# Reordering the first loads of a gated mixer kernel: first wk piece at the head of the ACT queue, gate vector second, and one transposed load in two parts

## The chip, the cores and the metric

The kernel runs on one NeuronCore of one Trainium2 chip. The metric is device time in microseconds (us) of a whole execution, as the median of several runs. Before the change it is 262.96 us (three runs, 262.92 to 263.25).

## What is computed

For x of 2048 rows and 640 columns in bfloat16 two blocks are computed and mixed row by row. Block A is a linear attention with 32 heads of 20 columns; block B is a layer norm, a product, a shift of four column groups along the rows, a second product and a two-layer MLP. Cut to what matters:

```python
g = sigmoid((x * gate_w).sum(-1, keepdims=True))
# A: linear attention, phi(t) = where(t > 0, t + 1, exp(t)) + 1e-6
q, k, v = heads(x @ wqkv)
kv = einsum("bhsd,bhse->bhde", phi(k), v);  z = phi(k).sum(rows)
a = (einsum("bhqd,bhde->bhqe", phi(q), kv) / (phi(q) . z + 1e-6)) @ wo
# B: mixer and MLP
h  = gelu(layernorm(x) @ w1)
x1 = x + shifted(h) @ w2
b  = x1 + gelu(layernorm(x1) @ w3) @ w4
out = g * a + (1 - g) * b
```

## The kernel before

The 2048 rows are 16 chunks of 128 rows (NCH), or 4 tiles of 512 (NT). The 640 columns are 5 pieces of 128 (DC). The whole program is one unrolled list with a schedule written out by hand: each engine does its instructions in the order in which the code names them, and semaphores between engines are put in by the framework.

The first stage, up to about 27 us, is the K product with phi. For it TensorE (PE) needs x transposed (xT, the stationary operand) and the five wk pieces (wk_sb, the moving operand). The chunks of xT come in two ways. Chunks 0 and 1 are loaded plainly (load_x, line 120) and transposed on PE by turn (lines 207 to 221): products with the identity for chunk 0, transposes for chunk 1, and a copy out of PSUM by VectorE (DVE), line 218. Chunks 2 to 15 are loaded by transposing DMAs (load_xT, line 123), six of them: chunks 2, 3, 4 to 5, 6 to 7, 8 to 11 and 12 to 15, all on the SP queue.

The gate needs the product of x with gate_w. It is had as one more column of the K product: gate_w is loaded as 5 rows of 128 (g5, line 129), copied by DVE into a zeroed tile (line 201), turned by one small product (line 217, inside turn(0)), and written into column 640 of wk_sb by DVE (line 221). The second half of each K product (hf = 1 in k_mm, line 185, 321 columns) reads that column; the first half (320 columns) does not.

The start is ordered by hand. Two queues issue loads: SP (nc.sync) and ACT (nc.scalar). SP has x chunk 0, wk pieces 1, 3 and 4, then the transposing loads, then wq, the rest of x, wv, w1, six pieces of wo, eight of w2, and w3 (lines 138 to 147). ACT has the gate vector, wk piece 0, x chunk 1 and wk piece 2. Meanwhile PE runs filler products on constants (warmup, line 198): six before turn(0), one after it, and one of 256 columns before the second and before the third wk piece of chunk 0. The wk pieces of chunk 0 are used in the order k0_order (line 192), that is 1, 0, 3, 4, 2, with turn(1) ahead of the fourth. Then the chunks 1 to 15 follow with the pieces in order (lines 232 to 235). Each chunk is evacuated by k_evac: ScalarE (ACT) copies the gate column (line 189) and takes exp (line 177), DVE finishes phi (lines 178 and 179).

The landings of the loads are told by eight semaphores that all DMAs take in turn; a DMA that takes one again waits first until the earlier one with it has landed. The trace shows the eight in this order at the start: gate vector, x chunk 0, wk 0, wk 1, x chunk 1, wk 3, wk 2, wk 4. The first six transposing loads take the first six of them again.

After the K product come the Q product (line 242, needs wq), K transposed times x (line 319), and the mixer and MLP stages (lines 353, 436, 467, 483, 518). w2_sb is first used at line 436.

Of the kernel before, what the change touches and what calls it, by code (L numbers as in the profile page):

```python
# [16 lines left out]
def kernel(  # L17
# [14 lines left out]
    P = 128  # L32
# [12 lines left out]
    CG = D // 4  # L45
# [25 lines left out]
    def pair():  # L71
        return ps.tile([P, 2, 512], F32, name="pp")
# [7 lines left out]
    w2_sb = const.tile([P, DC, D], BF16)  # L80
# [36 lines left out]
    sp, aq, gq = nc.sync, nc.scalar, nc.gpsimd  # L117

    def load_x(c0, c1, q=sp):
        q.dma_start(x_sb[:, c0:c1, 0:D], x2[c0 * P:c1 * P, :].rearrange("(c p) d -> p c d", p=P))  # L120

    def load_xT(c0, c1):
        sp.dma_start_transpose(xT[:, :, c0 * P:c1 * P], x2[c0 * P:c1 * P, :])

    def load_wk(q, dc):
        q.dma_start(wk_sb[:, dc, 0:D], A_wqkv[dc * P:(dc + 1) * P, D:2 * D])

    load_x(0, 1)
    aq.dma_start(g5[:], gate_w.rearrange("(c p) -> c p", p=P))
    load_wk(sp, 1)  # L130
    load_wk(aq, 0)
    load_x(1, 2, aq)
    load_wk(sp, 3)
    load_wk(aq, 2)
    load_wk(sp, 4)
    for c0, c1 in ((2, 3), (3, 4), (4, 6), (6, 8), (8, 12), (12, 16)):
        load_xT(c0, c1)
    sp.dma_start(wq_sb, wqkv_v[:, :, 0:D])
    load_x(2, 16)
# [1 line left out]
    sp.dma_start(w1_sb[:], B_w1.rearrange("(c p) f -> p c f", p=P))  # L141
    for g in range(NG):
        sp.dma_start(wo_sb[:, g, :], A_wo[row0[g]:row0[g] + P, :])
    for g in range(4):
        sp.dma_start(w2_sb[:, g, :], B_w2[CG * g:CG * g + P, :])
        sp.dma_start(w2_sb[32 * g:32 * (g + 1), 4, :], B_w2[CG * g + P:CG * (g + 1), :])
    sp.dma_start(w3_sb[:], B_w3.rearrange("(c p) f -> p c f", p=P))

# [40 lines left out]
        nc.scalar.copy(ylog[:, c:c + 1], pt[:, 1, HD:HD + 1])  # L189
        phi(pk[:, c, :].rearrange("p (h e) -> p h e", h=2), pt[:, :, 0:HD], D)  # L190

    k0_order = (1, 0, 3, 4, 2)
    warm = pair()
    one = nc.const_aps.tensor(1.0, (P, TS), BF16)

# [451 lines left out]
```

## Time and profile before

| what | us |
|---|---|
| median of three runs | 262.96 |
| the runs | 263.25, 262.96, 262.92 |
| profiled execution, whole time | 262.89 |
| its span, first to last instruction | 261.1 |
| PE busy in the span | 257.6 (99%) |
| DVE busy | 141.9 (54%) |
| ACT busy | 82.9 (32%) |
| POOL busy | 27.1 (10%) |

The span stands 1.8 us below the whole time of the same execution. The clock granted to PE is shown as full in every slice, and DMA engines are busy seven to nine tenths in the first four slices of 6.5 us. A line of the timeline has the start and the duration in us, the engine (PEld is PE's weight load, a q behind the name marks the issuing queue), the line of the code, the tiles written and read, and in brackets how long the engine stood idle before it and what ended that. "x6" means that six such instructions are drawn together.

### The profile page before, as it was taken

How to read it: one execution, taken by the hardware profiler on the slowest of the kernel's cores; microseconds unless marked ns; L12 is line 12 of the kernel's file. 1: busy time of each engine (PE TensorE's matmuls, PEld its weight loads, DVE VectorE, ACT ScalarE, POOL GpSimd, SP SyncE). 2: the span in 40 equal slices, each digit the busy share in tenths (PEclk: the TensorE clock that was granted, in tenths of full speed). 3: DMA queues.
4: the chain of work that ended last, by engine and by line, in shares of the span. 5: the costliest groups of instructions: out<-in, count | busy, mean ns of one | idle time of the engine just before them, and what ended most of it. 6: DMA issues, size and time to landing. Idle time of an engine off the chain costs nothing.

```text
span 261.1 us, 4172 instructions
## 1 busy us (share of the span) xinstructions
PE 257.6 (99%) x1670; PEld 159.1 (61%) x1670; DVE 141.9 (54%) x277; ACT 82.9 (32%) x124; POOL 27.1 (10%) x82
## 2 busy tenths in 40 slices
PE   8999999999999999999999999999999999999995
PEld 4777555788754644565676566567745567555543
DVE  2788778899947884967312378970312223112132
ACT  1555554321165346431520311140233350142100
POOL 3000050012220140131000123310000000000000
PEclk9999999999999999999999999999999999999999
DMA  7999987016684826996002011331200001100011
GB/s 205 179 204 377 365 241 306 0 28 126 125 99 88 220 54 145 207 298 60 0 3 75 25 28 25 75 54 25 78 25 0 0 3 50 53 0 0 0 53 50
DMA packets 47265, 25.78 MB, mean 99 GB/s; under 512 B 35214, under 2 KB 46478, under 8 KB 47246
## 3 DMA queue, kind: packets, MB, share of 16 engines
q1 hardware_dynamic: 46804, 25.03, 39.5%
q10 hardware_dynamic: 442, 0.49, 0.5%
q8 instruction: 13, 0.21, 0.4%
q14 instruction: 6, 0.05, 0.1%
HBM read 13.03 MB, written 3.60 MB: 64 GB/s over the span
## 4 chain that ended last, share of the span: by engine, by line
PE 99%; DVE 0%; issue 0%
PE pp L518 22%; PE pp L483 21%; PE pp L185 9%; PE pp L319 8%; PE pp L436 8%; PE pp L467 8%; PE pp L353 8%; PE pp L242 8%; PE pp L198 1%; PE pp L527 1%; PE pp L492 1%; PE pp L386 1%; PE pp L372 1%; PE pp L257 0%; PE pp L215 0%; DVE oc L532 0%
## 5 line engine op out<-in xcount | busy, mean ns | idle before, releaser
L483 PE MATMUL pp<-lnxT,w_sb 128*128 128x512 bf16 x260 | 60.0, 379 | 0.0
L518 PE MATMUL pp<-w_sb,h 128*128 128x384 bf16 (+3 forms) x416 | 57.9, 299 | 0.0
L485 ACT ACTIVATE h<-pp 128x1024 bf16<-128x1024 f32 (+1 forms) x28 | 27.0, 963 | 94.3 <-PE pp L483 94.3
L518 PEld LDWEIGHTS <-h 128*128 128x128 bf16 x416 | 38.3, 98 | 19.4 <-issue 1.2
L483 PEld LDWEIGHTS <-w_sb 128*128 128x128 bf16 x260 | 25.4, 98 | 27.2
L532 DVE SCALAR_TENSOR_TENSOR oc<-pp,omg,x 128x640 bf16<-128x640 f32 (+2 forms) x20 | 14.4, 748 | 45.4 <-PE pp L527 21.2
L470 DVE SCALAR_TENSOR_TENSOR x<-pp,gate,x 128x640 f32<-128x640 f32 x16 | 14.1, 879 | 33.6 <-PE pp L467 33.6
L177 ACT ACTIVATE e<-pp 128x640 bf16<-128x640 f32 (+1 forms) x26 | 21.5, 827 | 9.6 <-PE pp L242 9.6
L467 PE MATMUL pp<-m_sb,pqT 128*128 128x320 bf16 x160 | 24.3, 299 | 0.0
L436 PE MATMUL pp<-w_sb,hsT 128*128 128x320 bf16 x160 | 23.5, 299 | 0.0
L185 PE MATMUL pp<-wk_sb,xT 128*128 128x320 bf16 (+1 forms) x160 | 23.0, 302 | 0.0
L319 PE MATMUL pp<-x_sb,pk 128*128 128x320 bf16 (+1 forms) x160 | 22.0, 300 | 0.0
L242 PE MATMUL pp<-xT,hsT 128*128 128x512 bf16 x100 | 21.7, 379 | 0.0
L319 PEld LDWEIGHTS <-pk 128*128 128x128 bf16 x160 | 18.8, 117 | 3.2
L436 PEld LDWEIGHTS <-hsT 128*128 128x128 bf16 x160 | 15.6, 98 | 7.7
L467 PEld LDWEIGHTS <-pqT 128*128 128x128 bf16 x160 | 15.7, 98 | 7.7
L289 POOL TENSOR_SCALAR rstd<-mv 128x1 f32<-128x1 f32 (+1 forms) x20 | 7.7, 386 | 115.4 <-DVE mv L295 115.4
L185 PEld LDWEIGHTS <-xT 128*128 128x128 bf16 x160 | 15.6, 99 | 6.5 <-DVE xT L218 0.2
L439 DVE TENSOR_TENSOR x<-pp,x_sb 128x640 f32<-128x640 f32 x16 | 13.1, 816 | 10.6 <-PE pp L436 10.4
L353 PE MATMUL pp<-lnxT,w_sb 128*128 128x512 bf16 x80 | 18.1, 379 | 0.0
L242 PEld LDWEIGHTS <-hsT 128*128 128x128 bf16 x100 | 11.8, 118 | 9.7
L179 DVE SCALAR_TENSOR_TENSOR pk<-pp,e 128x640 bf16<-128x640 f32 x16 | 13.2, 825 | 1.7
(75 smaller groups left out, 191.1 us busy)
## 6 DMA issues: line engine op xcount, KB each, us to landing
x_sb<-in_A_x_dram SPq DMA_DIRECT2D x1, 2240.0 KB, 11.2
out_dram<-oc SPq DMA_DIRECT2D x14, 160.0 KB, 1.8
w_sb<-in_B_w_dram SPq DMA_DIRECT2D x1, 2160.0 KB
w_sb<-in_B_w_dram SPq DMA_DIRECT2D x1, 2080.0 KB, 11.7
wo_sb<-in_A_wo_dram SPq DMA_DIRECT2D x6, 160.0 KB, 7.3
m_dram<-x SPq DMA_DIRECT2D x3, 320.0 KB, 2.9
hsT<-in_A_wqkv_dram SPq DMA_DIRECT2D x1, 800.0 KB
m_sb<-in_A_wqkv_dram SPq DMA_DIRECT2D x1, 800.0 KB
```

The lines of the kernel that those rows point to most:

```text
L177: nc.scalar.activation(ev, src, ACT.Exp)
L185: nc.tensor.matmul(pt[:, hf, 0:n], lhsT=xT[:, dc, c * P:(c + 1) * P], rhs=wk_sb[:, dc, hf * HD:hf * HD + n], start=(dc == first), stop=(dc ...
L242: nc.tensor.matmul(pt[:, t % 2, :], lhsT=wq_sb[:, dc, :].rearrange("p (m j) -> p j m", j=DC)[:, j], rhs=xT[:, dc, t * TS:(t + 1) * TS], st ...
L319: nc.tensor.matmul(pt[:, hf, 0:HD + hf], lhsT=w, rhs=x_sb[:, c, hf * HD:(hf + 1) * HD + hf], start=(c == 0), stop=(c == NCH - 1))
L353: nc.tensor.matmul(pt[:, i, :], lhsT=w, rhs=lnxT[t][:, dc, :], start=(dc == 0), stop=(dc == DC - 1))
L436: nc.tensor.matmul(pt[:, hf, 0:HD], lhsT=hsT[:, fc, 2 + c * P:2 + (c + 1) * P], rhs=w2_sb[:, fc, hf * HD:(hf + 1) * HD], start=(fc == 0), ...
L467: nc.tensor.matmul(pt[:, hf, 0:HD], lhsT=pqT[:, j, c * P:(c + 1) * P], rhs=m_sb[:, j, hf * HD:(hf + 1) * HD], start=(j == 0), stop=(j == D ...
L470: nc.vector.scalar_tensor_tensor(x1, pt[:, :, 0:HD], gate[:, c:c + 1], x1, op0=ALU.mult, op1=ALU.add)
L483: nc.tensor.matmul(pt[:, k, :], lhsT=w3_sb[:, dc, fc * P:(fc + 1) * P], rhs=lnT[:, dc, :], start=(dc == 0), stop=(dc == DC - 1))
L485: nc.scalar.activation(h2[:, 2 * i * TS:(2 * i + n) * TS], pt[:].rearrange("p h e -> p (h e)")[:, 0:n * TS], ACT.Gelu_apprx_tanh)
L518: nc.tensor.matmul(dst, lhsT=st[t]["h2"][:, fc * TS + cc * P:fc * TS + (cc + 1) * P], rhs=w4_sb[:, fc, a:b], start=start and fc == 0, stop ...
L532: nc.vector.scalar_tensor_tensor(oc[:, a:b], src, omg[:, c:c + 1], st[t]["x1"][cc][:, a:b], op0=ALU.mult, op1=ALU.add)
```

## The change

The ACT queue begins with wk piece 0 instead of the gate vector, which becomes its second load. The order of the loads within SP's queue is the same as before, though their place in the program's text moves. The transposing load of chunks 8 to 11 becomes two, 8 to 9 and 10 to 11. The first two of the eight w2 loads that fill column groups 0 and 1 become one load with the same bytes. Chunk 0 uses wk piece 0 first and wk piece 1 second.

```diff
     load_x(0, 1)
+    load_wk(aq, 0)
+    load_wk(sp, 1)
     aq.dma_start(g5[:], gate_w.rearrange("(c p) -> c p", p=P))
-    load_wk(sp, 1)
-    load_wk(aq, 0)
+    load_wk(sp, 3)
     load_x(1, 2, aq)
-    load_wk(sp, 3)
+    load_wk(sp, 4)
     load_wk(aq, 2)
-    load_wk(sp, 4)
-    for c0, c1 in ((2, 3), (3, 4), (4, 6), (6, 8), (8, 12), (12, 16)):
+    for c0, c1 in ((2, 3), (3, 4), (4, 6), (6, 8), (8, 10), (10, 12), (12, 16)):
         load_xT(c0, c1)
...
+    sp.dma_start(w2_sb[:, 0:2, :], B_w2[0:2 * CG, :].rearrange("(g p) f -> p g f", g=2)[0:P])
     for g in range(4):
-        sp.dma_start(w2_sb[:, g, :], B_w2[CG * g:CG * g + P, :])
+        if g >= 2:
+            sp.dma_start(w2_sb[:, g, :], B_w2[CG * g:CG * g + P, :])
         sp.dma_start(w2_sb[32 * g:32 * (g + 1), 4, :], B_w2[CG * g + P:CG * (g + 1), :])
...
-    k0_order = (1, 0, 3, 4, 2)
+    k0_order = (0, 1, 3, 4, 2)
```

## The prediction, made before the result was known

> **What bounds the kernel now.** I read the busy shares first: PE is busy 257.6 of the 261.1 us span (99%). Then the chain of work that ended last, in order of time, because on such a kernel only a hole in PE's row, or a stretch at the lower clock, can be won or lost. Its start:
>
> ```profile
> 0.83 2.61 PE pp L198 x6
> 3.44 0.53 PE pp L215 x5
> 3.98 0.01 PE pp L217
> 3.98 0.45 PE pp L198
> 4.43 0.27 PE pp L185
> 4.70 0.03 issue
> 4.72 0.43 PE pp L185
> ...
> 6.01 0.28 PE pp L213 x5
> 6.29 21.09 PE pp L185 x154
> 27.38 21.58 PE pp L242 x100
> ```
>
> From 0.83 us to the end PE runs piece after piece. L198 is filler on constants, put where data is awaited. The change leaves each filler in place, so it removes no PE work: it can only close or open waits. Where they are is in the timeline of the first 26 us (start, duration, engine, line; in brackets the idle time before and its releaser):
>
> ```profile
> 0.79 0.57 ACTq L129 DMA_DIRECT2D g<-in_gate_w_dram  x1
> ...
> 2.65 13.64 SPq L123 DMA_TRANSPOSE xT<-in_A_x_dram  x6
> 2.72 0.18 DVE L201 COPY g5z<-g 5x128 bf16<-5x128 bf16 x1 [1.73 <-DMA g<-in_gate_w_dram]
> ...
> 3.06 0.65 PEld L215 LDWEIGHTS <-x_sb 128*128 128x128 bf16 x5 [0.42 <-DMA x_sb<-in_A_x_dram]
> ...
> 3.69 0.89 DVE L218 CAST xT<-pp 128x256 bf16<-128x256 f32 x2 [0.79 <-PE pp L215]
> ...
> 4.50 0.17 DVE L221 CAST wk_sb<-pp 128x5 bf16<-128x5 f32 x1
> ...
> 16.30 9.79 PEld L185 LDWEIGHTS <-xT 128*128 128x128 bf16 x73 [0.16 <-DMA xT<-in_A_x_dram]
> ```
>
> The reader is to see a chain of three arrivals: the gate vector g lets DVE copy it at 2.72; x chunk 0 lets PE load at 3.06; then casts, then L221, which writes the gate column. The second half of the first K product reads that column, and starts at 4.72, right after L221 ends at 4.67. The first half began at 4.22 and takes 0.27, so PE waits some 0.2 us there: the one hole of the start. At 16.30 chunk 8's weights come as its transfer lands, yet the single matmul records around it stay 0.135 us apart (16.05, 16.18, 16.32, 16.46): no hole, but no slack either.
>
> **What the Trainium skill says.** "TensorE: Matmul & The Clock Gate", Part 1, has the array at half rate until about 3.4 us of sustained work have passed. The trace agrees on the rates: 512-column fillers start 0.43 us apart (1.64, 2.06, 2.49), warm 320-column products 0.135. From the gaps between 5.15 and 5.33 the rate doubles near 5.29 us. "DMA: Bandwidth & Descriptors", section on queues, rings and completion order: SP and ACT have a ring each on the same 16 engines, and an engine drains a packet of one ring before it turns to the other. The packet records agree: after the first 160 KB piece, the pieces of both queues pass one after the other, alternating: wk1 (SP), wk0 (ACT, first row 3.19), wk3, x chunk 1, and so on. Two of g's five rows ran at 2.27, when x chunk 0's eight rows on those engines were through. The same page, on issuing engines, says a second queue saves only issue time; so wk0 beside x chunk 0 brings no bandwidth, it takes part of it.
>
> **The change, part by part.**
>
> *wk0 to the head of ACT.* It is issued at 0.79 with x chunk 0, where g was. A 160 KB piece is eight 1280-byte rows on each engine at 0.055 us, 0.44 us. The first touch of the weight tensor costs more: between 2.33 and 2.93 the records hold one slow row for most engines, 0.19 to 0.74 us, as wk1 starts; wk0 will pay that now. Two orders are possible, since the first rows of the two queues stood 0.07 us apart before (1.74 for g, 1.81 for x):
> (a) wk0's rows go ahead of x's on some engine. Then x lands at 3.02 (last landing record) + 0.44 + 0.2 to 0.7, or 3.7 to 4.2. Load and matmul follow within 0.1, and the filler ended near 3.28: PE and the casts are 0.5 to 1.0 us late.
> (b) x goes first. Then x is on time, but see g.
>
> *g second on ACT.* In (b) it stands behind wk0, perhaps wk1 too. The second ACT transfer had its first row at 3.19 before; one more piece makes 3.7. A landing came 0.31 us after its row (g: 1.74 and 2.05), so g lands at 3.5 to 4.0, not 2.62. The wait is L201's on DVE, with the L218 casts and L221 queued behind; L217 on PE waits for its copy, with the filler and every K product behind it. Copy start comes 0.1 after landing, its end 0.18 later: casts can start at 3.8 to 4.3 instead of 3.69, 0.1 to 0.6 late. Before, this wait was hidden under the arrival of x (2.90 against 3.06); that cover is what the move spends.
>
> I take 0.5 us late for either order; the ends are 0.1 and 1.0. Below zero isn't to be had here: x isn't issued earlier, and the hole before 4.72 ends with L221, behind the same casts.
>
> *What 0.5 us late costs.* The second half of the first product starts at 5.22 instead of 4.72. After 5.29 everything runs at the double rate. Until chunk 1's transposes are through, PE has: this half (0.17, part of it cold), filler 0.11, two products 0.27, filler 0.11, two products 0.27, five transposes 0.28. 5.22 + 1.21 = 6.43, against 6.29 before: **+0.14 us**. The idle half microsecond replaces cold work that is then done warm. With 0.1 late it is about +0.05 (half); with 1.0 late all of it is warm: 5.72 + 1.18 = 6.90, +0.6.
>
> *k0 order (0, 1, ...).* Same ten products. wk1 landed at 4.06, 0.16 ahead of its use at 4.22; wk0 takes that place, issued 0.45 us earlier. Without that margin a landing 0.3 late would cost 0.15 at the cold rate. In the trace it is covered: nothing.
>
> *Lanes on SP.* Eight landing semaphores serve all transfers in turn, and a transfer waits for the earlier one of its lane: the first transpose (chunk 2) shares g's, landed at 2.62, issued at 2.65. With wk0 at ACT's head I expect it to wait for wk0 instead, to 3.5 to 4.1. The other transposes, wq and x's bulk are queued behind. The last landings of the transposes were 7.10, 7.95, 9.81, 12.32, 16.26 and 18.34. With chunk 1 starting at 6.29 + 4 x 0.136 = 6.83 and 1.36 us per chunk, chunks 2, 3, 4, 6, 8 and 12 are wanted at 8.19, 9.55, 10.91, 13.62, 16.34 and 21.77: slack 1.1, 1.6, 1.1, 1.3, 0.1, 3.4. Transpose packets started only at 5.4, behind wk4, so most of the 0.9 to 1.5 us of later issue vanishes in that backlog. Nothing for all but chunk 8.
>
> *Split of chunks 8 to 11.* One more transpose issue, about 2 us for two chunks instead of 4.08 for four; SP has time (wq landed at 21.40, wanted at 27.38). Chunks 8 and 9 land near 14.3 instead of 16.26: it gives chunk 8 the slack that the later issue takes. In the profiled execution the gain is 0; uncovered, the late issue would cost up to 1 us there.
>
> *w2 in one transfer less.* One SP issue of 0.33 us less near 30 us, used from 85.97: nothing. With the split it keeps the number of transfers, so later lanes stay.
>
> Sum: +0.14. The profiled execution took 262.89 (261.1 span, 1.8 around it), which gives 263.03; it stands 0.07 below the median 262.96, so against the median it is **263.1**. A measurement of this kernel can tell about 0.2% from no change, 0.53 us: 262.43 to 263.49.
>
> **The rivals.**
> 1. *The moves change nothing on the path* (chance 0.20). x goes first and g goes ahead of wk1, landing by 3.4. For it: the casts need g only by about 3.4. Against: the second ACT transfer never started before 3.19. Time 262.9, or 262.8 if the hole before 4.72 shrinks.
> 2. *The clock comes a window later: slower* (0.14). Up to 5.29 PE idles about 0.2 us; with the change 0.6 to 0.7. If the monitor asks for more work than that leaves, the rate doubles 3.4 us later, by the clock page's window: 3.4 us at half rate lose 1.7 us. It decides at a threshold that no view shows. Against: the fillers still cover four fifths. Time 264.7.
> 3. *The transposes lose their backlog* (0.10). If SP's wait of up to 1.5 us passes through whole, chunk 2 or 4 lands 0.4 late on top of a start that is 1.0 late: 263.0 + 0.6 + 0.3, so 263.5 to 263.9. Against: packets before 5.4 were queued, not starved.
> 4. *Faster by more than can be told* (0.06). The three runs span 0.33 us; if that is chunk 8 or wk1 coming late without the profiler, the split and the order save it, and with the hole closed the time is 262.4. Against: the profiled execution, without such a wait, is already the fastest.
>
> **Numbers.** Forecast 0.50, of which 0.04 beyond 263.49 (1.0 late). Faster 0.06; same 0.46 + 0.20 = 0.66; slower 0.04 + 0.14 + 0.10 = 0.28. The range takes in the forecast with both ends, rivals 1 and 3: 262.5 to 263.9; left out are the clock and the gain, 0.20.
>
> **What would show it.** After the change the idle time before L215's load should grow from 0.42 to nearly 1 us, or L201's start should move from 2.72 past 3.6; L221 should end near 5.2; the first transpose issue should start after 3.3; no idle time before chunk 8's loads; chunk 1 should start near 7.0. L221 ending at 4.7 makes rival 1 right. A run of L185 products 0.27 apart after 5.5 makes rival 2 right. Idle time at chunks 2 to 7 is rival 3. I am wrong altogether if PE's fillers or products end earlier than now.

## The result, and the profile after

The changed kernel takes 263.84 us (median of five runs, 263.67 to 264.21) against 262.93 of the kernel before on the same chip (five runs, 262.70 to 263.25): ratio 1.0033, 95% interval 1.002 to 1.0047. Measured twice more (c1 and e1 below), each time beside the kernel before, it gave 1.0014 (1.0001 to 1.0027) and 1.0033 (1.0016 to 1.0051). The time lies in the stated range, but the forecast was +0.14 us and no measurable change; it is +0.9 us here and +0.5 and +0.6 in the repeats, slower. The runs of one kernel scatter over about 1 us, with a few beyond.

The profiled execution took 264.21 us, its span 262.5. The profile before, of 262.89 us, is of a quick execution: of 145 later runs of that kernel 10 were as quick, and their median was 263.24. So the two profiles differ by more than the two kernels do in the median. In the changed code the gate load is line 131 instead of 129, and the lines of the computing part stand two later (L185 is L187, L215 is L217, L218 is L220, L221 is L223). The timeline of its first 26 us:

```profile
0.79 0.40 ACTq L126 DMA_DIRECT2D wk_sb<-in_A_wqkv_dram  x1
...
0.79 0.40 SPq L120 DMA_DIRECT2D x_sb<-in_A_x_dram  x1
...
1.21 0.58 ACTq L131 DMA_DIRECT2D g<-in_gate_w_dram  x1
...
3.83 14.43 SPq L123 DMA_TRANSPOSE xT<-in_A_x_dram  x7
3.92 0.18 DVE L203 COPY g5z<-g 5x128 bf16<-5x128 bf16 x1 [2.94 <-DMA g<-in_gate_w_dram]
4.05 0.45 PEld L217 LDWEIGHTS <-x_sb 128*128 128x128 bf16 x5 [1.41 <-DMA x_sb<-in_A_x_dram]
...
4.49 0.89 DVE L220 CAST xT<-pp 128x256 bf16<-128x256 f32 x2 [0.38 <-PE pp L217]
...
5.29 0.17 DVE L223 CAST wk_sb<-pp 128x5 bf16<-128x5 f32 x1
```

Each arrival is later: g's copy 2.72 to 3.92, x's load 3.06 to 4.05, the casts 3.69 to 4.49, the gate column 4.50 to 5.29. The landing records say the same: wk 0 at 3.82, g at 3.82, x chunk 0 at 4.00 (3.02 before). Here wk 0's rows went ahead: ACT's ring had its first row at 1.82 and 14 rows started before SP's first at 2.04. The first transposing load was issued at 3.83, right after wk 0 landed.

The chain of waits for the first 20 us:

```profile
0.79 3.21 DMA x_sb<-in_A_x_dram
4.00 0.05 issue
4.05 0.72 PE pp L217 x5
...
5.51 0.43 PE pp L187
5.94 0.21 PE pp L200
6.15 0.53 PE pp L187 x2
6.69 0.21 PE pp L200
6.90 0.53 PE pp L187 x2
7.43 0.30 PE pp L215 x5
7.74 12.26 PE pp L187 x90
```

Before, the chain ran over PE's fillers from 0.83; now its first 4 us are the load of x. And the pieces after it are slow: two products take 0.53 as late as 6.90. Before, two took 0.27 already here:

```profile
5.36 0.27 PE pp L185 x2
```

The rate doubled near 7.3, not near 5.3. Of the +1.34 us at the start of chunk 1 (6.78 before, 8.12 now, by single records) 0.79 came with the data: the first product started at 5.01 instead of 4.22. The other 0.55 came with the clock. Nothing is given back later: the whole time less the start of chunk 1 is 256.11 us before and 256.09 after. In all profiles below that reach full rate by then, but one (a6), it is 256.06 to 256.11, so the start of chunk 1 is the quantity to explain.

### The profile page after: what moved, and what is told of

Its sections match the earlier page's. It is cut to its first block, busy times and chain, and to the rows that moved or that the text cites. A ratio compares the mean times of both kernels' runs of the same rounds, so it can differ in the third digit from the quotient of the medians.

```text
span 262.5 us, 4153 instructions
## 1 busy us (share of the span) xinstructions
PE 257.3 (98%) x1652; PEld 159.4 (61%) x1670; DVE 141.9 (54%) x277; ACT 82.8 (32%) x124; POOL 26.7 (10%) x82
## 4 chain that ended last, share of the span: by engine, by line
PE 97%; DMA 1%; issue 0%; DVE 0%
PE pp L520 22%; PE pp L485 21%; PE pp L187 9%; PE pp L321 8%; PE pp L438 8%; PE pp L469 8%; PE pp L244 8%; PE pp L355 8%; DMA x_sb<-in_A_x_dram 1%; PE pp L529 1%; PE pp L494 1%; PE pp L388 1%; PE pp L374 1%; PE pp L259 0%; PE pp L200 0%
## 5 line engine op out<-in xcount | busy, mean ns | idle before, releaser
L187 PE MATMUL pp<-wk_sb,xT 128*128 128x320 bf16 (+1 forms) x160 | 23.5, 306 | 0.0
L187 PEld LDWEIGHTS <-xT 128*128 128x128 bf16 x160 | 15.8, 100 | 6.4 <-DVE xT L220 0.2
```

The lines of the kernel that those rows point to most:

```text
L187: nc.tensor.matmul(pt[:, hf, 0:n], lhsT=xT[:, dc, c * P:(c + 1) * P], rhs=wk_sb[:, dc, hf * HD:hf * HD + n], start=(dc == first), stop=(dc ...
```

## The experiments

In the diffs below, lines are those of the kernel named first. "Full rate" is read from the gaps between single matmul records.

**a1_gate_first: the changed kernel with the ACT order of before.**

```diff
+    aq.dma_start(g5[:], gate_w.rearrange("(c p) -> c p", p=P))
+    load_wk(sp, 1)
     load_wk(aq, 0)
-    load_wk(sp, 1)
-    aq.dma_start(g5[:], gate_w.rearrange("(c p) -> c p", p=P))
```

> The changed kernel with the gate vector back at the head of the ACT queue and wk piece 0 second; the split, the w2 merge and the piece order (0, 1, ...) stay. Theory A (wk piece 0 ahead of x chunk 0 on the DMA engines makes x late, and the idle PE also gets its full clock later): x lands near 3.0 us again, no idle time before the first transposes, full rate near 5.3; 262.9 to 263.1 us, at most 0.1 to 0.2 over the kernel before, because the first product now waits for wk piece 0, which landed at 4.37 before and is used at 4.22. Theory B (the loss comes from the other edits: the split, the later transposes, the piece order): stays near 263.8.

Measured: 263.26 us, ratio 0.9997 (0.9982 to 1.0013). x landed at 2.96. The loss is gone when the two loads on ACT are swapped back; split, w2 merge and piece order don't cost it. Its profile also shows what the new piece order risks, on PE's timeline:

```profile
3.84 0.59 PE L200 MATMUL pp<-const-bfloat16-1.0 128*128 128x512 bf16 x1
5.13 0.43 PE L187 MATMUL pp<-wk_sb,xT 128*128 128x320 bf16 x2 [0.70 <-DMA wk_sb<-in_A_wqkv_dram]
```

wk 0, wanted first and issued second on ACT, landed at 5.09. Here the rate had doubled by 5.13 already (two products in 0.43), so the moment at which the clock changes differs between executions.

**a2_swap_only: the kernel before with the ACT order changed, nothing else.**

```diff
+    load_wk(aq, 0)
+    load_wk(sp, 1)
     aq.dma_start(g5[:], gate_w.rearrange("(c p) -> c p", p=P))
-    load_wk(sp, 1)
-    load_wk(aq, 0)
```

> The kernel before with only the ACT order changed: wk piece 0 first, gate vector second. Theory A: x chunk 0 lands near 4.0, full rate near 7.3, the whole loss of the change: 263.7 to 264.0. On top of it chunk 8 may wait, since the four-chunk transpose is issued about 1 us later and PE is only 0.8 to 1.4 late itself: 0 to 0.3 more. Theory B: 262.9 to 263.1.

Measured: 263.99, ratio 1.003 (1.0015 to 1.0044): the change's own loss. x landed at 4.11. Six of 22 runs are beyond 264.2, and the profiled one, 265.26, is one of them:

```profile
4.15 0.71 PE L215 MATMUL pp<-ident,x_sb 128*128 128x128 bf16 x5 [0.71 <-DMA x_sb<-in_A_x_dram]
...
6.79 0.74 PE L185 MATMUL pp<-wk_sb,xT 128*128 128x320 bf16 x2
7.33 0.74 PE L213 MATMUL pp<-ident,x_sb 128*128 128x128 bf16 x5
```

Two products in one group show 0.74 at half rate and 0.43 to 0.44 at full rate. Here they are slow past 7, and full rate came near 9.4. Chunk 8 did not wait: its single transposing load landed at 17.02, before PE came to it.

**c1_after_again and e1_after_beside: the changed kernel, unedited, measured again twice.**

> The changed kernel once more, to be compared with the kernels of this call and to see a second profile. Theory A: x chunk 0 lands 0.9 to 1.1 later than in the kernel before, PE idle 0.6 to 0.7 us ahead of the transposes, the full rate anywhere from 6 to 9.5 us; ratio to before 1.002 to 1.004, 0.5 to 1.1 us. Should the full rate come as early as in the kernel before (near 5.3) and the loss be the same, the clock has no part in it.

> The changed kernel beside its variant with more filler, on one chip. So far its median stood 0.49 to 0.91 us over the kernel before, and its two profiles differ: in one the full rate came at 7.3 and PE's own work at half rate set the start of chunk 1 (8.1); in the other it came near 5.2 and the landing of the last wk pieces set it (7.6). I expect 0.5 to 0.9 over before again.

Measured: 263.73, ratio 1.0014 (1.0001 to 1.0027), and 263.76, ratio 1.0033 (1.0016 to 1.0051). Their profiled executions took 263.69 and 263.44, and full rate came near 5.2 and 4.3, as early as in the kernel before or earlier. They are still slower than it. The chain of waits of c1 tells why:

```profile
2.18 4.87 DMA wk_sb<-in_A_wqkv_dram
7.05 0.04 issue
7.09 12.97 PE pp L187 x94
```

The chain no longer goes through x: it is wk 4, landing at 7.05. PE had waited for wk 3 before (landed 6.22) and then stood until 7.09. In e1 wk 4 landed at 6.77. In the kernel before it landed at 6.01 and wk 2, the last piece, at 6.47. So there is a second way to the same loss: with the swap the last first-stage pieces are late too. In seven profiles, with and without the swap (before, a1, b1, c1, d1, e1, e2), chunk 1 starts 0.31 to 0.37 us after the last piece has landed.

**a3_more_filler and e2_filler_beside: the changed kernel with filler up to the landing of x.** Both are the same kernel.

```diff
-    warmup(5)
-    warmup(1, 3 * P)
+    warmup(7)
+    warmup(1, 2 * P)
```

> The changed kernel with more filler ahead of x chunk 0: seven products of 512 columns and one of 256 instead of five and one of 384, so that PE works until 4.03 us, where x lands. It does more PE work than the changed kernel. Theory A, clock part: PE is no longer idle, the full rate comes near 5.3 as before, what follows x runs warm: chunk 1 starts 0.4 later than in the kernel before, not 0.8 to 1.4: 263.2 to 263.4, that is 0.4 to 0.6 less than the change. Rival (the clock comes at a time of its own, whatever PE did): the same time as the changed kernel, 263.7 to 264.0.

> The variant with more filler again (0.34 us over before the first time), now in the same call as the changed kernel. If PE's gap ahead of x takes part in the loss through the clock, it is 0.2 to 0.5 under the changed kernel, with fewer runs beyond 264.2. If the landing of the last wk pieces alone sets the typical run, the two medians agree within 0.1.

Measured: 263.62, ratio 1.0011 (0.9996 to 1.0026), then 263.70 beside 263.76 of the changed kernel, ratios 1.0022 (1.0014 to 1.003) and 1.0033. The medians agree within 0.1; over all measurements none of 27 runs with filler lies beyond 264.2 (highest 264.11), and five of 37 of the changed kernel do (highest 265.51). So no part of PE's gap ahead of x shows in the typical loss. It may make the long runs, but the counts are small, and the kernel before, which in its profile has no such gap, has nine beyond 264.2 in 145. PE stays busy up to the landing of x in the profile of e2, and then waits for its last pieces (wk 4 at 6.89):

```profile
4.05 0.63 PE L217 MATMUL pp<-ident,x_sb 128*128 128x128 bf16 x5
...
6.41 0.44 PE L215 MATMUL pp<-ident,x_sb 128*128 128x128 bf16 x5
6.93 3.16 PE L187 MATMUL pp<-wk_sb,xT 128*128 128x320 bf16 x22
```

Five transposes that start at 6.41 are through within 0.3 of it at this rate (0.28 in the chain of before), and the next product starts at 6.93.

**a4_less_filler and a6_small_gap: the kernel before with less filler, the loads untouched.**

```diff
-    warmup(5)
-    warmup(1, 3 * P)
+    warmup(4)        # a4
+    warmup(5)        # a6
```

> The kernel before with less filler: four products of 512 columns ahead of the transposes and not the one of 384 and the fifth, so that PE is idle from 2.54 us to the landing of x near 3.05. All loads as before, less PE work, and the transposes can start 0.2 earlier than before. Theory A, clock part: the idle half microsecond moves the full rate 1 to 2 us later, which costs 0.3 to 0.9: 263.2 to 263.8. Rival (the clock doesn't follow such a gap): 262.8, 0.1 less than before.

> The kernel before without the filler of 384 columns, so that PE idles only from 2.96 to about 3.1 us. With the run of four fillers only (0.67 idle) the full rate came at 8.3 and the median ratio was 1.002. Theory (a clock window with up to some tenth of idle time still counts as busy): no loss, 0.9995 to 1.0005, full rate at 4 to 7. Rival (any gap ahead of x starts the count again): [...]a ratio of 1.001 to 1.002.

Measured: a4 263.63, ratio 1.0021 (1.0004 to 1.0037), eight of 22 runs beyond 264.2; a6 263.35, ratio 1.0007 (0.9991 to 1.0023). Less work made a4 slower though x landed at 3.17 and the last pieces at 6.24 and 6.42. Its PE timeline in the profiled run (264.2):

```profile
3.21 0.72 PE L214 MATMUL pp<-ident,x_sb 128*128 128x128 bf16 x5 [0.52 <-POOL bmask L163]
...
5.85 0.74 PE L185 MATMUL pp<-wk_sb,xT 128*128 128x320 bf16 x2
6.39 0.74 PE L212 MATMUL pp<-ident,x_sb 128*128 128x128 bf16 x5
6.92 3.14 PE L185 MATMUL pp<-wk_sb,xT 128*128 128x320 bf16 x17
```

There is no wait for data between 4.9 and 8, only half rate, until 8.3. That is the share of the clock by itself. (The releaser named in the bracket is only the last event the profile saw; the weight load beside it waits for x.) For a6 full rate came near 5.7; its interval tells it apart neither from the kernel before nor from a loss of 0.2%. It is the one profile that lost time after the start of chunk 1 (256.53): 0.1 at chunk 8 and 0.36 near 76 us, in a later stage.

**d2_x_second: the kernel before with x chunk 0 behind wk piece 1 on SP.**

```diff
-    load_x(0, 1)
+    load_wk(sp, 1)
     aq.dma_start(g5[:], gate_w.rearrange("(c p) -> c p", p=P))
-    load_wk(sp, 1)
+    load_x(0, 1)
```

> The kernel before with x chunk 0 issued second on SP, behind wk piece 1; the gate vector stays first on ACT, the transposes stay as they were, and no two full pieces start together. x should land at 3.5 to 4.0, as in the changed kernel, but the last wk pieces should land as in the kernel before (6.3 to 6.9). Theory X (what costs is that x is late and PE idle): the loss of the change, ratio 1.002 to 1.0035. Theory L (what costs is that the last wk pieces land later when two pieces start together, and the late x mostly hides behind that): less than half of it, 1.0003 to 1.0012.

Measured: 265.59 (six runs, 263.26 to 266.92), ratio 1.0082 (1.005 to 1.0115). Both theories missed. x landed at 4.52, later than I meant, g in time, the last pieces at 6.17 and 6.60.

```profile
4.57 0.71 PE L215 MATMUL pp<-ident,x_sb 128*128 128x128 bf16 x5 [1.12 <-DMA x_sb<-in_A_x_dram]
...
7.74 0.74 PE L213 MATMUL pp<-ident,x_sb 128*128 128x128 bf16 x5
8.27 2.02 PE L185 MATMUL pp<-wk_sb,xT 128*128 128x320 bf16 x7
```

With PE idle for some 1.3 us and nothing else late, full rate came at 10.1. The profiled execution took 265.82, 2.9 us more than the profile before: 1.30 came with the data (first product at 5.52 instead of 4.22), the rest with the clock. A late x alone thus cost 2.3 us in the median, the larger part through the clock by this split; five of the six runs are 264.96 or longer.

**a5_x1_first: x chunk 1 in wk 0's place at the head of ACT.**

```diff
-    load_wk(aq, 0)
+    load_x(1, 2, aq)
     load_wk(sp, 1)
     aq.dma_start(g5[:], gate_w.rearrange("(c p) -> c p", p=P))
     load_wk(sp, 3)
-    load_x(1, 2, aq)
+    load_wk(aq, 0)
...
-    k0_order = (0, 1, 3, 4, 2)
+    k0_order = (1, 0, 3, 4, 2)
```

> The changed kernel with x chunk 1 at the head of the ACT queue, gate vector second, wk piece 0 third; piece order (1, 0, ...) as before. The same 160 KB stand beside x chunk 0, but from tensor x. Theory A1 (bytes and the slow first touch of the weights both delay x chunk 0): x lands near 3.4 to 3.5, by the bytes alone (0.44), not 4.0; 263.2 to 263.5. Theory A2 (two full pieces that start together are slow, whatever they read): x lands near 4.0, 263.7 to 264.0. In both the gate vector lands past 3.3.

Measured: 265.67 (six runs), ratio 1.0082 (1.0057 to 1.0108). x landed at 3.59 and g at 3.70. The time itself says nothing on the question: wk 0, now third on ACT, landed at 6.50, PE waited 1.0 us for it, and full rate came at 9.4. The landing lies between A1 and A2. With wk 0 beside it x landed at 3.68 to 4.11 (six profiles). Against 3.02 before that is 0.66 to 1.09 later; 0.57 came, in this one profile, with a full piece of x in its place. What the slow first rows add stays open, and they aren't the weights' own: in a3's profile the slow rows at 1.8 to 2.1 (0.35 to 0.77) were x's.

**b1_wk2_on_sp and d1_split_only: two tries for a better version.**

```diff
# b1, from the kernel before
     load_wk(sp, 3)
-    load_wk(aq, 2)
     load_wk(sp, 4)
+    load_wk(sp, 2)
# d1, from the changed kernel
+    aq.dma_start(g5[:], gate_w.rearrange("(c p) -> c p", p=P))
+    load_wk(sp, 1)
     load_wk(aq, 0)
-    load_wk(sp, 1)
-    aq.dma_start(g5[:], gate_w.rearrange("(c p) -> c p", p=P))
...
-    k0_order = (0, 1, 3, 4, 2)
+    k0_order = (1, 0, 3, 4, 2)
```

> A try for a better version: the kernel before with wk piece 2 moved from the end of the ACT queue to SP, behind wk piece 4 and ahead of the transposing loads. In the profile of before PE waits 0.11 us at 6.4 for this piece, which landed at 6.47 while the first transposes ran beside it from 5.4. If the transposes hold it up, it lands 0.1 to 0.3 earlier and the kernel gains 0.1 (ratio 0.9996); if the bytes of all pieces set it, it lands at the same time, and the transposes, issued 0.45 later, may leave chunk 8 waiting up to 0.4: 263.0 to 263.6.

> The kernel before with only the split of the transposing load of chunks 8 to 11 and the merged w2 load; ACT order and piece order as before. In one profile of a kernel with the old single transfer (small gap) the start was quick, chunk 1 began at 6.55, and chunk 8 then waited some 0.4 us for its transfer, which landed at 16.40. Theory: the split pays whenever the start is quick and costs nothing else: chunks 8 and 9 land near 13 to 14.5, no wait; ratio to before 0.9985 to 0.9997, 0.1 to 0.4 us faster. Rival: chunk 8 seldom waits, or the seventh transpose pushes something else: 0.9998 to 1.0003.

Measured: b1 263.23, ratio 1.0005 (0.9997 to 1.0013); d1 263.17, ratio 0.9994 (0.9983 to 1.0005). Neither is told apart from the kernel before. In b1 wk 2 landed at 6.83, not earlier. The ground given for d1 was misread: in a6's profile chunk 1 began at 6.82, not 6.55, and chunk 8 waited about 0.1:

```profile
16.44 1.61 PEld L185 LDWEIGHTS <-xT 128*128 128x128 bf16 x13 [0.26 <-DMA xT<-in_A_x_dram]
```

In d1 chunks 8 and 9 landed at 13.21 instead of 16.26, so the split does give slack; before, that slack was seldom wanted.

## Why the prediction was wrong in its sum, though the time lies in its range

*That the time lies in the range is luck.* The sum reached at most 263.6, with its end of 1.0 us late. Up to 263.9 the range was drawn for rival 3, the transposes, which did not occur.

*x beside wk 0: later, as said.* In the first profile x was the later arrival, in c1 it was g (3.87 against 3.68, copy at 3.97, casts at 4.16). I took 0.5 late; the casts were 0.80 late in the first profile and 0.47 in c1, within the bounds 0.1 to 1.0. But order (b), x first and then on time, never occurred: in c1 and e1 x's ring had its first row first (1.82 against 2.01, 1.83 against 1.95), and x still landed at 3.68 and 3.92. No run delays g alone, so its share in the later casts is read from these profiles only.

*"After 5.29 everything runs at the double rate": this step failed in the first profile.* The sum refunded the idle time with a clock moment copied from one execution. The moment isn't fixed. With x and g ahead and the filler of before, full rate came at 5.3 (before), 5.8 (d1), 6.1 (b1) and by 5.13 (a1); in the unedited changed kernel at 7.3, 5.2 and 4.3. In the first profile the sign named for rival 2, products 0.27 apart after 5.5, is there; it cost 0.55 us, not 1.7. That spread fits "TensorE: Matmul & The Clock Gate", Part 1, of the Trainium skill, which has a free-running window of about 3.4 us. With PE's idle time taken from the starts of its single records, e1's last window would be 0.9 to 4.3 with 0.74 us idle, c1's 1.8 to 5.2 with 0.72. In a4 the one before the last, 1.4 to 4.9, had 0.90 idle and didn't count; in the first profile the one before the last, 0.5 to 3.9, held 1.0 and didn't count. A limit between 0.74 and 0.90 would explain these. It is inferred from four profiles, not shown. So rival 2, the clock, is real: it set the first profile and those of a2, a4 and d2, all of them 264.2 us or longer.

*The hole I did not see.* I wrote that the start has one hole. The single records of before have another: the product that starts at 6.27 is followed at 6.51 by the next, 0.11 us more than its 0.136, for wk 2, which had landed at 6.47. The chain drew it as one piece of 154 products. So the start of chunk 1 hung on the last landing as well, and the sum had no term for that: this is the step that failed for the typical run. The last piece landed at 7.16, 7.26 and 7.04 in the three profiles of the changed kernel, 6.90 to 7.45 in the other three with the swap, and at 6.28 to 6.90 in six without it and with x ahead: 0.53 later on average, against a loss of 0.5 to 0.9 in the medians. That PE waits for the last pieces (for wk 4, the last but one) is shown in c1, e1 and e2; that this makes the typical loss is inferred from these, since no run moves the last pieces alone. Why they are late is open. The slow start (first rows of 0.4 to 0.6 us on ACT's ring) doesn't explain it: by 3.0 us the plain loads had moved 232 KB, against 216 before. They fell behind only after 4.0, to 796 KB against 907 by 5.0.

*The rest held, as far as it could be seen.* The first transpose waited for wk 0 (3.83); the other transposes took that up in their backlog (chunk 2 landed at 7.73, wanted at 9.5); chunks 8 and 9 landed at 14.24 against 17.6 wanted: no wait, so rival 3 didn't occur. No cost of the w2 merge and the split shows (d1). The forecast of +0.14 rested on a refund that came neither from the clock in the first profile nor from the data in c1 and e1.

## What to carry to other kernels

Where a start is bound by loads, a transfer put beside the one that is awaited first doesn't come for free: here both the first and the last arrival came later, by 1.0 and 0.7 us in the first profile. Look up the landing time of every piece that the first stage reads, since a chain drawn in merged pieces hides a wait of a tenth of a microsecond, and that is the next bound. Treat the moment at which PE gets its full rate as a spread over several executions, and keep PE fed with filler up to the first arrival: that didn't better the median here, but it may end the runs that were 1 to 2 us longer (none of 27, against five of 37).

## What I had not expected of the hardware

The same kernel had its full rate at 4.3, 5.2 and 7.3 us in three executions. And less work was slower: one filler of 512 columns and one of 384 fewer (a4) cost 0.2% (1.0004 to 1.0037), though x landed at 3.17 and the last pieces by 6.42.
